# The fetch of the first pair's k, moved to the head of ScalarE's queue

## The chip, the cores and the metric

One core of one Trainium2 chip runs the whole kernel. The time is the device time of one execution in microseconds; lower is better.

## What is computed

Causal attention over 2 batches of 12 heads (448 positions, head dimension 64), then a gated layer and a hard-swish layer over the 896 rows of 768 that the attention gives. Cut to what matters:

```
scores = q @ k.T / sqrt(64);  scores above the diagonal = -1e9
attn   = exp(scores - max) / (sum + 1e-9)
x      = (attn @ v), heads side by side            # 896 x 768
x      = (sigmoid(x @ w_gate) * (x @ w_val)) @ w_out
h      = x @ w_in
out    = (h * clip(h + 3, 0, 6) / 6) @ w_out2
```

All inputs and the output are float32.

## The kernel before

The heads are handled in 12 pairs (6 for each batch). A pair p has its q, k and v fetched by `load(p, nm)` (L235); q and k come as two transfers each, one for each head, 112 KB every one, into a ring of three buffers (L246, L248). `t_pe` (L256) turns q and k by four transposes each on TensorE (L260) into PSUM; `t_out` (L267) copies them to SBUF, q on ScalarE with the scale (L270), k on VectorE (L272). The transposed q and k of all pairs share one PSUM buffer, except that the k of pair 0 goes to the buffer "pav" (L258). `s_pe` (L274) makes the scores: small mask products (L285), then the products s (L293), in two groups for each pair; `s_max`, `s_exp`, `s_rcp`, `s_nrm` are the softmax on VectorE, ScalarE and GpSimd; `c_pe` turns the probabilities (L347), and `d_pe` multiplies them with v (L367).

All engines take their instructions in the order in which the program names them. That order is a list of steps with planned times (`AT`, `SHIFT`, `OWN`, L397 to L422), sorted by `emit_in_order` (L515). Every transfer of q, k and v is issued by SP's queue, except pair 0's k, which is issued by ScalarE's (L248). In the planned order that step (`Lk` of pair 0) stands behind the scaling of pair 0's q (`Thq` of pair 0, L270). The steps Z (`z_pe`, L455) are products of ones into a PSUM tile that nobody reads; nine of them stand at the very beginning of TensorE's order (listed at L456 in the rows below), the others between the steps of the first pairs.

On SP's queue the order at the opening is: q of pairs 0, 1, 2, k of pair 1, q of pair 3, k of pair 2, v of pair 0, then on by pair; the first weights of the gated layer (`load_unit`, L98, L103) come after the v of pair 2. Their decoding begins with `dec_scale` (L113, L115) on ScalarE.

After the attention the gated layer (L190, L708) and the hard-swish layer (L190, L1161) follow, with weights fetched on SP's queue as buffers come free and decoded on ScalarE and VectorE; some of their split parts are made by transfers that GpSimd issues (L144).

Of the kernel before, what the change touches and what calls it, by code (L numbers as in the profile page):

```python
# [31 lines left out]
def kernel(  # L32
# [178 lines left out]
    with tc.manual_schedule():  # L211

        with ExitStack() as actx:
# [19 lines left out]
            live = {}  # L233

            def load(p, nm):  # L235
                b, hp = divmod(p, NPAIR)
                if nm == "v":
                    for j in range(2):
                        chunks = v[b, 2 * hp + j].rearrange("(c p) d -> p c d", p=D)
                        for x in range(2):  # L240
                            nc.sync.dma_start(
                                out=vs[p % NV][x * D : (x + 1) * D, x != j :, j],
                                in_=chunks[:, x != j :: 2],
                            )
                    return
                t = p_raw.tile([CP, S // CP, 2, D], F32, tag=nm, name=nm)  # L246
                for j in range(2):
                    (nc.scalar if (p, nm) == (0, "k") else nc.sync).dma_start(  # L248
                        out=t[:, :, j, :],
                        in_=(q if nm == "q" else k)[b, 2 * hp + j].rearrange(  # L250
                            "(c p) d -> p c d", p=CP
                        ),
                    )
                live[nm, p] = t
# [170 lines left out]
            for p in range(NP):  # L425
                def add(key, after, fn, *args):
                    steps.append(((p, key), [(p, a) for a in after], fn, (p, *args)))

                for nm in ("q", "k", "v"):
                    add("L" + nm, [], load, nm)  # L430
                for nm in ("q", "k"):
                    add("T" + nm, ["L" + nm], t_pe, nm)
                    add("Th" + nm, ["T" + nm], t_out, nm)
                for i, ts in enumerate(STILES):
                    add(f"S{i}", ["Thq", "Thk"], s_pe, ts)
                    for t in ts:
                        add(f"M{t}", [f"S{i}"], s_max, t)
                for ts in STILES:
                    for t in ts:
                        add(f"E{t}", [f"M{x}" for x in ts], s_exp, t)  # L440
                for i, ts in enumerate(STILES):
                    add(f"Q{i}", [f"E{t}" for t in ts], s_eps, i)
                    add(f"R{i}", [f"Q{i}"], s_rcp, i)
                    for t in ts:
                        add(f"N{t}", [f"R{i}"], s_nrm, t)
                for g in range(NG):
                    tiles = [f"N{t}" for t in range(GROUPS[g][0][0], NQ)]
                    add(f"C{g}", tiles, c_pe, g)
                    add(f"H{g}", [f"C{g}"], c_out, g)
                for d, gs in enumerate(DSTEPS):  # L450
                    add(f"D{d}", [*(f"H{g}" for g in gs), "Lv", *[f"D{d - 1}"][: d]], d_pe, d)
                add("Xh", [f"D{len(DSTEPS) - 1}"], x_hi)
                add("Xl", ["Xh"], x_lo)
# [61 lines left out]
            def emit_in_order():  # L515
# [19 lines left out]
                for key in sorted(left, key=lambda key: (when(key), key)):  # L535
                    _, fn, args = left[key]
                    fn(*args)

            ones = nc.const_aps.tensor(1.0, [P, 512], BF16)
            idle_ps = ps_pt.tile([P, 512], F32, tag="pt", name="pt")  # L540
            make_identity(nc, identf)
# [686 lines left out]
```

## Time and profile before

| what | us |
|---|---|
| median of three runs | 590.04 |
| lowest and highest run | 589.8, 591.88 |
| the profiled execution | 589.66 |
| its span, first to last instruction | 587.9 |

| engine | busy us | share of the span |
|---|---|---|
| TensorE | 573.8 | 98% |
| its weight loads | 506.1 | 86% |
| VectorE | 450.6 | 77% |
| ScalarE | 325.1 | 55% |
| GpSimd | 88.1 | 15% |

All times in the rows below are of the profiled execution, counted from the start of its span. In the profile PE is TensorE's products, PEld its weight loads, DVE is VectorE, ACT is ScalarE, POOL is GpSimd and SP is SyncE; SPq and ACTq are the issuing of transfers by those queues. L248 is line 248. Matmuls are pipelined and their ends are modelled, so neighbours may overlap by a little.

### The profile page before, as it was taken

Reading aid. Unit: us, or ns where it says so; the run is one execution under the profiler, and the core shown is the slowest. Engines: PE = TensorE matmul, PEld = TensorE weight load, DVE = VectorE, ACT = ScalarE, POOL = GpSimd, SP = SyncE. Lnnn points to the kernel's source line nnn. Section 1 sums busy time; section 2 is a strip of 40 time slices with the busy share of each in tenths; the row PEclk is TensorE's granted clock in tenths of the full one; section 3 lists DMA queues with packets and bytes.
Section 4 is the critical chain, followed back from the end, with each engine's and each line's share of the span. In section 5 each row is a group of like instructions: output and inputs, shape, how many; then the busy total and the mean of one; then the engine's idle time right before and its main releaser. Section 6 shows DMA issues by size and latency. Waiting matters only on the chain.

```text
span 587.9 us, 8611 instructions
## 1 busy us (share of the span) xinstructions
PE 573.8 (98%) x3252; PEld 506.1 (86%) x3253; DVE 450.6 (77%) x673; ACT 325.1 (55%) x619; POOL 88.1 (15%) x146
## 2 busy tenths in 40 slices
PE   6999999999999999999999999999999999999997
PEld 3666666899998999889999999988899899899997
DVE  1778995588778889889767887898999888867601
ACT  1988986454747565577343223777776644433200
POOL 0545455012201111110000000113122000000000
PEclk7999999999999999999999999999999999999999
DMA  7645625069848776761334533577988333338002
GB/s 150 155 118 132 146 67 177 2 157 216 212 131 193 180 208 168 198 180 31 108 115 154 162 107 108 145 179 187 216 191 224 94 107 110 107 109 255 0 3 92
DMA packets 86921, 82.21 MB, mean 140 GB/s; under 512 B 35680, under 2 KB 77408, under 8 KB 86880
## 3 DMA queue, kind: packets, MB, share of 16 engines
q1 hardware_dynamic: 79904, 64.27, 37.0%
q0 software_dynamic: 6048, 17.17, 15.9%
q8 instruction: 25, 0.41, 0.3%
q10 hardware_dynamic: 928, 0.23, 0.2%
q14 instruction: 16, 0.13, 0.1%
HBM read 61.73 MB, written 2.75 MB: 110 GB/s over the span
## 4 chain that ended last, share of the span: by engine, by line
PE 55%; DVE 29%; ACT 10%; issue 4%; DMA 2%; ACTq 0%; DVEq 0%
PE m L1161 17%; PE w L708 11%; PE m L190 10%; DVE b L128 5%; PE pav L367 5%; PE s L293 4%; PE pt L347 4%; DVE b L134 4%; DVE lo L158 3%; DVE b L124 3%; ACT hi L153 2%; ACT b L115 2%; PE tr L260 2%; DVE g L182 2%; DVE raw L120 2%
## 5 line engine op out<-in xcount | busy, mean ns | idle before, releaser
L1161 PE MATMUL m<-hi,g 128*128 128x384 f32 x448 | 114.3, 335 | 0.7 <-DVE g L1129 0.7
L153 ACT CAST hi<-b 128x768 fp32r<-128x768 f32 x36 | 29.8, 836 | 104.3 <-DVE b L134 96.3
L1161 PEld LDWEIGHTS m<-hi,g 128*128 128x128 f32 x448 | 80.8, 188 | 1.5 <-DVE g L1129 1.3
L1161 PE MATMUL m<-lo,g 128*128 128x384 f32 x224 | 74.9, 335 | 0.4 <-DVE lo L158 0.4
L708 PE MATMUL w<-T,hi 128*128 128x448 f32 x252 | 72.0, 367 | 1.4 <-ACT g2r L725 1.4
L190 PE MATMUL m<-g,hi 128*128 128x448 f32 x288 | 70.1, 365 | 0.0
L128 DVE SCALAR_TENSOR_TENSOR b<-b,raw 128x768 int32<-128x768 int32 x68 | 65.3, 960 | 2.3
L134 DVE SCALAR_TENSOR_TENSOR b<-raw,b 128x768 int32<-128x768 int32 x68 | 65.3, 960 | 2.4
L115 ACT ACTIVATE b<-raw 128x768 f32<-128x768 f32 x68 | 61.3, 905 | 0.0
L190 PEld LDWEIGHTS m<-g,hi 128*128 128x128 f32 x288 | 54.1, 188 | 4.3
L124 DVE TENSOR_SCALAR b<-b 128x768 f32<-128x768 f32 x68 | 37.9, 557 | 25.7 <-ACT b L115 25.3
L158 DVE TENSOR_TENSOR lo<-b,hi 128x768 fp32r<-128x768 f32 x36 | 34.2, 956 | 27.4 <-ACT hi L153 27.2
L337 POOL TENSOR_SCALAR pr<-pr,rc 128x192 f32<-128x192 f32 (+3 forms) x96 | 46.1, 497 | 53.0 <-DVE rc L329 43.9
L708 PEld LDWEIGHTS w<-T,hi 128*128 128x128 f32 x252 | 47.1, 188 | 5.9 <-ACT g2r L725 1.8
L190 PE MATMUL m<-x,hi 128*128 128x448 f32 x192 | 49.1, 368 | 0.0
L708 PE MATMUL w<-T,lo 128*128 128x448 f32 x126 | 46.3, 368 | 0.7 <-DMA lo<-S 0.5
L317 ACT ACTIVATE pr<-s,nm 128x192 f32<-128x192 f32 (+3 forms) x96 | 44.5, 476 | 3.7 <-DVE nm L305 3.2
L144 POOL DMA_DIRECT2D lo<-S x26 | 24.9, 956 | 131.4 <-ACT lo L143 111.2
L1161 PEld LDWEIGHTS m<-lo,g 128*128 128x128 f32 x224 | 42.0, 188 | 0.7 <-DVE lo L158 0.7
L305 DVE TENSOR_REDUCE nm<-s 128x2 f32<-128x384 f32 (+3 forms) x48 | 30.7, 681 | 14.9 <-PE s L293 14.5
L190 PE MATMUL m<-g,lo 128*128 128x448 f32 x144 | 41.0, 366 | 0.0
L190 PEld LDWEIGHTS m<-x,hi 128*128 128x128 f32 x192 | 35.7, 188 | 3.1 <-issue 0.4
(127 smaller groups left out, 1054.7 us busy)
## 6 DMA issues: line engine op xcount, KB each, us to landing
raw<-in_moe_w_out_dram SPq DMA_DIRECT2D x28, 768.0 KB, 4.4
raw<-in_moe_w_in_dram SPq DMA_DIRECT2D x16, 768.0 KB, 4.7
lo<-S POOLq DMA_DIRECT2D x26, 384.0 KB, 4.2
raw<-in_moe_w_gate_dram SPq DMA_DIRECT2D x12, 768.0 KB, 5.1
raw<-in_moe_w_val_dram SPq DMA_DIRECT2D x12, 768.0 KB, 5.3
q<-in_q_dram SPq DMA_DIRECT2D x24, 112.0 KB, 2.9
g<-b POOLq DMA_DIRECT2D x7, 384.0 KB, 6.5
k<-in_k_dram SPq DMA_DIRECT2D x22, 112.0 KB, 4.0
```

The source lines that it names most:

```text
L115: nc.scalar.activation(b, words(u)[0].bitcast(F32), AF.Copy, scale=REBIAS)
L124: nc.vector.tensor_scalar(b, b, UPPER_MAX, -UPPER_MAX, op0=ALU.min, op1=ALU.max)
L128: nc.vector.scalar_tensor_tensor(bi, bi, 3, words(u)[1], op0=ALU.logical_shift_left, op1=ALU.bitwise_or)
L134: nc.vector.scalar_tensor_tensor(bi, words(u)[0], -(2 ** 31), bi, op0=ALU.bitwise_and, op1=ALU.bitwise_or)
L153: nc.scalar.copy(hi, part_t[u])
L158: nc.vector.tensor_sub(lo, part_t.pop(u), split_t[u][0].bitcast(F32))
L190: nc.tensor.matmul(ps[:, b, :S], lhsT=w[a][:, i * P : (i + 1) * P], rhs=x(c, k0 + i, b), start=(first and i == 0 and n == 0), stop=(last a ...
L305: nc.vector.tensor_reduce(nm, live["s", p, t], axis=AX.X, op=ALU.max, negate=True)
L317: nc.scalar.activation(to if j else to[:, ::-1], ps[:, j].rearrange("p (c d) -> p c d", d=D), AF.Exp, bias=nm[:, j : j + 1], accum_out=sm[ ...
L337: nc.gpsimd.tensor_scalar(pr[:, j], pr[:, j], rc[:, j : j + 1], 1.0, op0=ALU.mult, op1=ALU.mult)
L708: nc.tensor.matmul(ps, lhsT=w[a][:, k * P : (k + 1) * P], rhs=x[:, c, i], start=(first and i == 0 and n == 0), stop=(i == HK - 1 and n == ...
L1161: nc.tensor.matmul(po[t], lhsT=g2[2 * s + i][a][:, t * P : (t + 1) * P], rhs=w[e][:, i * HC : (i + 1) * HC], start=(s == 0 and i == 0 and ...
```

## The change

`load` returns at once when the asked q or k tile is already live, and pair 0's k is loaded ahead of everything else that the attention part emits, before the constants are made and before the planned order begins. When the planned step for it comes, it does nothing. The issuing queue is ScalarE's, as before.

```diff
@@ -234,6 +234,8 @@
             def load(p, nm):
                 b, hp = divmod(p, NPAIR)
+                if (nm, p) in live:
+                    return
                 if nm == "v":
@@ -536,6 +538,7 @@
                     _, fn, args = left[key]
                     fn(*args)
 
+            load(0, "k")
             ones = nc.const_aps.tensor(1.0, [P, 512], BF16)
             idle_ps = ps_pt.tile([P, 512], F32, tag="pt", name="pt")
             make_identity(nc, identf)
```

## Rows read from the trace of the kernel before

**Rows 1.** The page's forty slices: TensorE's busy tenths and its granted clock.
```profile
PE   6999999999999999999999999999999999999997
...
PEclk7999999999999999999999999999999999999999
```

**Rows 2.** Chain that ended last, 0 to 18 us: start us, us, what.
```profile
0.78 3.58 PE pt L456 x9
4.36 0.48 PE tr L260 x4
...
5.36 4.02 DMA k<-in_k_dram
...
9.42 1.01 PE tr L260 x4
10.43 0.43 PE pt L456
10.86 0.75 PE tr L260 x4
11.60 0.43 PE s L285 x8
12.04 1.87 PE s L293 x8
13.90 0.60 PE tr L260 x4
...
14.73 1.06 PE s L293 x8
...
16.49 0.81 PE pt L456 x3
...
17.32 0.35 PE s L285 x8
17.67 0.95 PE s L293 x8
```

**Rows 3.** Stretches of one us: busy us by engine, granted clock, DMA share, GB/s.
```profile
4.00:5.00 1.00, 0.82 (x6) 0.39 (x4) 0.00 (x0) 0.14 (x1) 0.00 (x0) 1.00 0.88 199
...
7.00:8.00 1.00, 0.00 (x0) 0.00 (x0) 0.00 (x0) 0.00 (x0) 0.00 (x0) 0.60 1.28 287
...
13.00:14.00 1.00, 1.00 (x5) 0.17 (x2) 0.05 (x1) 0.00 (x0) 0.00 (x0) 0.50 0.67 151
14.00:15.00 1.00, 1.00 (x16) 0.86 (x18) 1.00 (x2) 0.00 (x0) 0.00 (x0) 0.99 0.99 222
```

**Rows 4.** Timeline: start us, us, engine, line, operation, output<-input, count [idle before, releaser].
```profile
0.74 1.28 ACT L270 ACT_TABLE_LOAD   x1 [0.74 <-PEq L1212]
...
3.84 1.02 SPq L248 DMA_DIRECT2D k<-in_k_dram  x2
...
4.87 0.99 ACTq L248 DMA_DIRECT2D k<-in_k_dram  x2
...
10.47 0.62 DVE L272 COPY kt<-tr 128x448 f32<-128x448 f32 x1 [7.25 <-PE tr L260]
...
22.00 0.61 SPq L103 DMA_DIRECT2D raw<-in_moe_w_gate_dram  x1
...
34.09 0.91 ACT L115 ACTIVATE b<-raw 128x768 f32<-128x768 f32 x1
```

**Rows 5.** Transfers, single ones: count, KB each, us to landing (last row: median).
```profile
q<-in_q_dram SPq DMA_DIRECT2D x1, 112.0 KB, 2.9
...
k<-in_k_dram SPq DMA_DIRECT2D x1, 112.0 KB, 3.3
k<-in_k_dram ACTq DMA_DIRECT2D x1, 112.0 KB, 3.6
...
raw<-in_moe_w_gate_dram SPq DMA_DIRECT2D x12, 768.0 KB, 5.1
```

**Rows 6.** Waits for transfers, 15 to 588 us, longest: total us, times, longest us.
```profile
PEld w L708 <- DMA lo<-S: 0.9, 1, 0.9
```

## The prediction

> **What bounds the kernel now.** I read the page's forty slices first. TensorE's granted clock is full in every slice but the first, and the first is also the only slice, apart from the end, in which TensorE is less than 90% busy [rows 1]. So the place to look is the opening, 14.7 us long, and the views for it are the chain that ended last, the one-microsecond stretches, and the timeline of the queues.
>
> The chain of the opening [rows 2] reads: nine warm-up products to 4.36, the four transposes of pair 0's q (0.48 us), the scaling of qt on ScalarE, then 4.02 us of one transfer, the second half of pair 0's k, and only at 9.42 the transposes of that k. From there the chain is TensorE without a hole, step after step, into the first products s (L293) and on into pair 1 and pair 2. That transfer is late for one reason: ScalarE's queue issues k's two halves at 4.87, in 0.99 us, right when the ScalarE instruction that stands before them starts, and that one waits for q's transposes [rows 4]. ScalarE's own work until then is one table load at 0.74 [rows 4].
>
> The second thing to see is the clock. In the stretch 7 to 8 us, where TensorE does nothing, the mean granted clock is 0.60, and 14 to 15 has 0.99; 13 to 14 still 0.50, and 4 to 5 reads full [rows 3]. Half is the 1.2 GHz level, full the 2.4 GHz level. The warm-up products had ended in a full clock, as q's transposes (0.48 us) against k's (1.01 us) show [rows 2]; the engine then stood idle for 4.6 us and lost it, and did the first 4.5 us of work, from 9.42 to 13.90, at half.
>
> **The change part by part.** (1) Two transfers of 112 KB are issued at the head of ScalarE's queue instead of behind the scaling of qt; the planned load of that tile then returns at once, since it is live. No instruction is added or taken away. The issue costs 0.99 us of ScalarE's queue [rows 4], from 0.74 to 1.73. The table load (1.28 us) then runs to about 3.0, and ScalarE's next instruction needs q's transposes, which end at 4.84 [rows 2]; so this costs nothing, and would cost only if q's transposes ended before 3.0. GpSimd and SP issue nothing later for it. SP's queue is not passed by any other transfer of its own, but its first ones now share the DMA engines with k.
>
> (2) When k lands. The second half is issued at 0.74 + 0.49 = 1.23. Lower bound: the second half of pair 0's q, issued at about the same time on SP with an empty machine, took 2.9 us [rows 5], so 4.1. Upper bound: the same transfer of before, with SP issuing beside it as now, took 4.02 us [rows 2] (its first half 3.6 [rows 5]), so 5.25. By sharing, q itself may slip by as much. In the good case q's transposes run as before and k's start right behind them, at 4.85; in the bad case both inputs land at 5.25, q's transposes take 0.5 to 0.6, and k's start at 5.85. Neither row is clearly nearer (the first has the empty machine, the second the two queues), so I take the middle, 5.3. Against 9.42 that is **4.1 us** off the path (3.6 to 4.6).
>
> (3) What the clock gives. With k there, TensorE's hole shrinks from 4.6 us to under 1 us, and I expect the clock to stay full. Then the chain from 9.42 to 13.90 [rows 2] runs at the durations that the same groups have after 14 us: transposes 0.60 instead of 1.01 (k) and 0.75 (pair 1's q); one warm-up product 0.27 (0.81 for three) instead of 0.43; mask products 0.35 instead of 0.43; eight products s 0.95 instead of 1.87. That is 2.77 instead of 4.48, so **1.7 us** more. VectorE's copy to kt (0.62 us [rows 4]) lies beside it: it ends 0.60 + 0.66 = 1.26 after k's transposes start, and the products s want it after 0.60 + 0.27 + 0.60 + 0.35 = 1.82. If the clock is not kept, this term is nothing.
>
> (4) What is late next. Pair 1's k, which SP issues from 3.84 [rows 4]. Its second half, issued about 4.36, took 3.3 us [rows 5] and lands at 7.7; its transposes would be due at 5.3 + 2.77 = 8.1. It fits with 0.4 to spare; at 4.02 us it would land at 8.4 and cost 0.3. Everything later on SP has more room. As the worst case, the first gate weights, were they issued no earlier than now (22.00) [rows 4], land after 5.1 [rows 5] at 27.7, and ScalarE's first use of them, at 34.09 now, comes at 28.3 [rows 4].
>
> (5) Whether the shift reaches the end. All engines take their work in order and every step of pair 1 stands behind one of pair 0; there is no later wait of TensorE on a transfer from memory. The longest wait on any transfer after 15 us is 0.9 us, and it is for a copy that GpSimd issues inside the GLU [rows 6], which moves with the rest. So the sum is 4.1 + 1.7 = 5.8 us, all of it on the path: 589.66 - 5.8 = 583.9 for the profiled execution (span 587.9 and 1.8 around it). That execution lies 0.4 below the median of the runs, 590.04, from which the forecast is **584.2**; its own range is 583.2 to 584.7, from 3.6 + 1.7 to k1 just in time (5.8 + 1.0).
>
> One rule of the Trainium skill speaks against a part of this. The rows show 199 GB/s between 4 and 5 us, with SP's queue at work almost alone, and 287 GB/s between 7 and 8, with ScalarE's beside it [rows 3], so a second queue did move more. The page "DMA: Bandwidth & Descriptors", section "Issuing engines are not separate DMA queues", says that transfers of all engines run on the same 16 DMA engines and interleave, so that issuing from several saves only sequencer time. By that rule q and k of pair 0 would slow each other; this is the first rival.
>
> **The rivals.** *The two fetches slow each other.* If two queues move no more than one, k's 224 KB beside q's cost 1.1 us at 199 GB/s [rows 3], q lands at 4.1 + 1.1 = 5.2 and k's transposes start at 5.85: 3.6 + 1.7 = 5.3 off, **584.7**. For it: q and k compete from the first byte. Against it: the 287 GB/s.
>
> *The clock falls all the same.* Between 4.4 and 8 us TensorE does transposes, one warm-up product and the first products s, with small holes, and not the dense work that it had before 14 us. If it runs at half from k's transposes on, as now, only term 2 is won: 590.04 - 4.1 = **585.9**. For it: no row of before shows a full clock through such a thin stretch. Against it: from 15 us on the chain has the same steps and the clock stays [rows 1].
>
> *The change doesn't do what it says.* The table load could stay ahead of the two issues, for its place is not written in the code. Then k is issued 1.28 us later [rows 4], lands at 5.4 to 6.5, and some 1.1 us of the gain is gone: **585.3**.
>
> *The wait is hidden anyway.* Some transfer or engine that does not depend on pair 0 sets a later point, and all of the shift is given back there: **590.0**. Against it stands the absence of any long wait on a transfer after 15 us [rows 6].
>
> *Slower.* The clock falls early, and the thin opening, no longer followed by 4.5 us of dense work, does not lift it for two pairs. At half rate a group of products s costs about 0.9 more (1.87 against 0.95) and four transposes about 0.4 more [rows 2]; a pair has two of each, so 2.6. The 4.1 us of term 2 are eaten when half rate outlasts the rest of pair 0 (one s and one transpose group, 1.3) and the whole of pair 1 (2.6); through pair 2 as well it would be 1.3 + 2.6 + 2.6 = 6.5 lost, 590.04 - 4.1 + 6.5 = **592.4**. Against it: half rate has ended here after 4.6 us of work.
>
> **How the numbers follow.** Forecast 584.2: 0.53. Fetches slow each other, 584.7: 0.15. Clock falls, 585.9: 0.16. Table load first, 585.3: 0.07. Hidden, 590.0: 0.05. Slower, 592.4: 0.04. The range 583.2 to 586.5 takes in the first four with their bounds and leaves out 0.09 above and a little below. A measurement of this kernel can tell about 0.5%, 2.95 us, from no change: faster 0.91, within 0.5% 0.05, slower 0.04.
>
> **What would show it.** Step 1: k's two issues at 0.74 on ScalarE's queue, ahead of the table load. Step 2: k's transposes between 4.85 and 5.85. Step 3: a granted clock of 1.00 in every stretch from 5 to 15 us, the first eight products s in about 1 us and ending near 8. Step 4: no wait for pair 1's k. Step 5: the later pairs spaced as now, all 5.8 us earlier, and the chain's other rows unchanged. I am wrong in the size if the clock row reads half there, and wrong in the matter if later pairs stand where they stood.

## The result, and the profile after

On the chip of the prediction's runs the changed kernel takes 583.76 us (median; 583.12 to 584.82) against 590.25 before: a ratio of 0.9887, interval 0.9862 to 0.9912. The profiled execution takes 583.4 against 589.66. The forecast was 584.2.

The chain of the opening in the changed kernel, start us, us, what; it answers to [rows 2]:

```profile
0.74 3.19 DMA k<-in_k_dram
...
3.94 0.39 SPq L250
...
4.37 3.79 DMA k<-in_k_dram
...
8.30 0.57 PE tr L262 x4
...
10.15 0.53 PE tr L262 x4
...
11.91 0.95 PE s L295 x8
```

The 4.02 us of pair 0's k are gone from the chain. In their place stands another k, pair 1's: its second half is issued at 4.37, lands after 3.79 us, and its transposes start at 8.30. In the kernel before they started at 13.90, so the chain is 5.60 us earlier there, and 5.76 at the first products s of pair 1 (11.91 against 17.67). By the first two links, SP's issue of pair 1's k waited for the landing of pair 0's first half of k. The trace bears this out: the issue waits on the semaphore that tells of this landing, and goes out 0.02 us behind it. It costs nothing here: the second half, for which the transposes wait, is issued at 4.37, and was issued at 4.38 in the kernel before.

The timeline of the same stretch, columns as in [rows 4]:

```profile
0.74 1.01 ACTq L250 DMA_DIRECT2D k<-in_k_dram  x2
0.78 4.00 PE L458 MATMUL pt<-const-bfloat16-1.0 128*128 128x512 bf16 x9 [0.78 <-PEq L1215]
1.78 1.28 ACT L272 ACT_TABLE_LOAD   x1 [1.78 <-issue]
4.60 0.98 PE L262 MATMUL tr<-identf,q 112*128 112x112 f32 x4
5.38 0.92 PE L262 MATMUL tr<-identf,k 112*128 112x112 f32 x4
6.35 0.55 PE L262 MATMUL tr<-identf,q 112*128 112x112 f32 x4
7.01 1.13 PE L295 MATMUL s<-kt,qt 64*128 64x192 f32 x8
8.30 0.57 PE L262 MATMUL tr<-identf,k 112*128 112x112 f32 x4 [0.15 <-DMA k<-in_k_dram]
```

Pair 0's k is issued first of all on ScalarE's queue, with the table load behind it. Its transposes follow q's directly, at 5.38. The first four transposes of q and of k take 0.98 and 0.92 us, which is half rate, and from 6.35 on the same group takes 0.55: in this execution the clock rose at about 6.1, where in the profiled execution of before it had risen by 4.3. The eight products s take 1.13 instead of some 2 us.

Stretches of one us, columns as in [rows 3]:

```profile
5.00:6.00 1.00, 1.00 (x8) 1.00 (x7) 0.00 (x0) 0.38 (x1) 0.00 (x0) 1.00 1.32 217
7.00:8.00 1.00, 1.00 (x16) 0.64 (x10) 0.00 (x0) 0.47 (x1) 0.00 (x0) 1.00 1.20 207
13.00:14.00 1.00, 1.00 (x7) 0.45 (x6) 1.00 (x2) 1.00 (x6) 0.90 (x2) 1.00 0.83 187
```

TensorE is busy throughout but for the 0.15 us before pair 1's k, and the clock column stays at 1.00 where before it read 0.50 from 7.2 to 14. It reads 1.00 in 5 to 6 as well, while the transposes ran at half rate: ahead of the first change that it records, the column shows no level to be trusted.

Whether the shift reaches the end is read from the 68 decoding steps of VectorE on L128, which are spread over the whole kernel. The first, the 26th and the 27th of them, in the kernel before:

```profile
44.41 0.96 DVE L128 SCALAR_TENSOR_TENSOR b<-b,raw 128x768 int32<-128x768 int32 x1
...
257.75 0.96 DVE L128 SCALAR_TENSOR_TENSOR b<-b,raw 128x768 int32<-128x768 int32 x1
...
279.37 0.96 DVE L128 SCALAR_TENSOR_TENSOR b<-b,raw 128x768 int32<-128x768 int32 x1
```

and in the changed kernel:

```profile
38.65 0.96 DVE L128 SCALAR_TENSOR_TENSOR b<-b,raw 128x768 int32<-128x768 int32 x1
...
251.94 0.96 DVE L128 SCALAR_TENSOR_TENSOR b<-b,raw 128x768 int32<-128x768 int32 x1
...
273.19 0.96 DVE L128 SCALAR_TENSOR_TENSOR b<-b,raw 128x768 int32<-128x768 int32 x1
```

The shift is 5.76 at the first, 5.81 at the 26th and 6.18 at the 27th; it stays between 6.18 and 6.27 up to the last. So between these two traces 5.76 us come from the opening, nothing of it is given back, and 0.4 more appears in one stretch of the gated layer that the change does not touch. That stretch turns up in the experiments.

### The profile page after: what moved, and what is told of

Same layout as the page of the kernel before. It is cut to its first block, busy times and chain, and to the rows that moved or that the text cites. A ratio compares the mean times of both kernels' runs of the same rounds, so it can differ in the third digit from the quotient of the medians.

```text
span 581.6 us, 8612 instructions
## 1 busy us (share of the span) xinstructions
PE 572.2 (98%) x3253; PEld 505.4 (87%) x3253; DVE 450.5 (77%) x673; ACT 324.8 (56%) x619; POOL 88.4 (15%) x146
## 4 chain that ended last, share of the span: by engine, by line
PE 58%; DVE 28%; ACT 8%; issue 3%; DMA 2%; SPq 0%; ACTq 0%; DVEq 0%; POOLq 0%
PE m L1164 17%; PE w L711 15%; PE m L190 10%; DVE b L128 5%; PE pav L369 5%; PE pt L349 4%; PE s L295 4%; DVE b L134 4%; DVE lo L158 3%; DVE b L124 3%; ACT hi L153 2%; DVE g L182 2%; ACT b L115 2%; DVE raw L120 2%; PE tr L262 1%
## 5 line engine op out<-in xcount | busy, mean ns | idle before, releaser
L128 DVE SCALAR_TENSOR_TENSOR b<-b,raw 128x768 int32<-128x768 int32 x68 | 65.3, 960 | 2.3
```

Source lines behind the costliest of these rows:

```text
L128: nc.vector.scalar_tensor_tensor(bi, bi, 3, words(u)[1], op0=ALU.logical_shift_left, op1=ALU.bitwise_or)
```

## The experiments

In what follows "the first step" is the start of the first L128 step. It measures the opening alone: 44.41 in the kernel before, 38.65 in the changed one.

**The changed kernel again.**

> The changed kernel again, as the reference for the other runs on the same chip. Its first trace had pair 0's k transposed from 5.38 us and pair 1's k from 8.30, with a wait of 0.15 us for the transfer of pair 1's k. If the time of the opening is set by that transfer (theory), pair 1's k is again transposed within 0.2 us of 8.3, whatever the clock does before, and the time is 583 to 585. If it is set by the clock and the products (rival), an execution whose clock rises sooner has it up to 1 us earlier.

584.31 us (583.33 to 584.43) against 589.56 for the kernel before on that chip, ratio 0.9910 (0.9896 to 0.9923). The first step is at 38.73 and pair 1's k is transposed from 8.29. The clock rose late here too (q's transposes 0.98 us), so theory and rival were not told apart. The stretch between the 26th and the 27th step of L128, however, differs from the first trace of the very same code:

```profile
252.09 0.96 DVE L128 SCALAR_TENSOR_TENSOR b<-b,raw 128x768 int32<-128x768 int32 x1
...
274.24 0.96 DVE L128 SCALAR_TENSOR_TENSOR b<-b,raw 128x768 int32<-128x768 int32 x1
```

It is 22.15 us here and was 21.25 there. Up to it the two executions differ by 0.15 us, behind it by 1.05. Against the first trace of the kernel before, the shift is 5.68 at the first step here and 5.36 at the last. The medians differ likewise: they fell by 6.49 us on the first chip and by 5.25 on this one. So the opening has to be read from the opening, not from the total time.

**The kernel before, a second trace.**

> The kernel before once more, for a second trace of its opening. If the moment at which the clock first rises differs between executions of the same code (theory, from the traces so far: q's transposes took 0.57 us for four in the first trace of before and 0.95 to 0.98 in three others), then either q's transposes again take 0.57 and end at 4.8, with k's at 9.4, or they take 0.95 and end at 5.5, with k's at 10.0; the time from there to the first eight products s of pair 1 is 8.0 to 8.4 in both, since TensorE then stands idle for over 4 us. Rival (the moment is fixed by the code): 4.8 and 9.4 again.

One execution, 590.63 us. In its chain:

```profile
4.78 0.64 PE tr L260 x4
...
5.44 0.39 ACT qt L270
...
5.87 4.00 DMA k<-in_k_dram
...
9.91 1.01 PE tr L260 x4
...
12.53 1.87 PE s L293 x6
...
18.34 0.95 PE s L293 x8
```

The moment of the first rise does differ between executions of one code. Here q's transposes took 0.83 us and ended at 5.42, so the scaling of qt, the issue of k behind it and k's transposes came 0.5 us later than in [rows 2]; the first step is at 45.05, 0.64 later. From k's transposes to pair 1's first products s it is 8.43 us (8.25 in the first trace, 8.0 to 8.4 expected), at half rate again. In the kernel before, then, a late clock delays the fetch; in the changed one it cannot. Against this trace the changed kernel's opening is 6.40 us earlier. The stretch of the gated layer is 21.24 us here and was 21.62 in the first trace.

**Only the clock: the gap filled, the fetch where it was.**

```diff
+            WARM += [-76841.5] * 18
             OWN.update({f"Z{i:02}": at for i, at in enumerate(WARM)})
```

> The kernel before, with the fetch of pair 0's k where it was, but 18 more idle products put between q's and k's transposes of pair 0, so that TensorE doesn't stand still for 4.6 us. Only the clock's term is tried. Theory: k's transposes still start at 9.4, the clock reads full from there on, the stretch from them to pair 1's k takes 2.8 to 3.0 us instead of 4.48, and the time is 1.5 to 1.7 below the kernel before, 588.6. Rival: the clock is worth nothing, since the data sets the pace of the opening: same time as before. A second rival: the filling overruns the landing of k and eats the gain.

> The kernel before with the 18 idle products in the gap, for a second trace, to see whether the opening's gain is steady and where it was lost. Theory: from k's transposes to the first eight products s of pair 1 again 6.2 us, 2.0 less than in the kernel before; decoding steps up to 250 us are 1.4 to 2.0 earlier than in the kernel before, by one constant shift; what the time then shows differs by up to 0.8 because the 108 products of the gated layer's last pair take 22.2 to 23.3 us from one execution to the next. Rival: the idle products make the gated layer slower, and the shift shrinks in every trace of this kernel by 0.5 or more.

In the first trace of it the chain reads:

```profile
6.01 3.99 DMA k<-in_k_dram
...
10.04 0.61 PE tr L260 x4
...
11.53 1.00 PE s L293 x8
...
16.27 0.95 PE s L293 x8
```

From k's transposes to pair 1's first products s it is 6.23 us, and 6.22 in the second trace (16.11 - 9.89): 2.0 less than 8.25 and 2.2 less than 8.43. The clock term is real in the opening. The filling itself did not get in the way: its products ended at 9.50 and 9.76, before k landed at 10.00 and 9.85. But k's transposes came late, at 10.04 and 9.89, since the clock rose late in both executions, and the first step is at 43.02 and 42.85: 1.4 to 1.6 before the first trace of before, 2.0 to 2.2 before the second. The time does not show it: 589.25 (587.79 to 592.44) against 589.56, ratio 0.9995 (0.9980 to 1.0009); the one execution of the second trace took 588.98. Part of the loss is in the same stretch, 22.08 and 22.02 us here. That is no longer than the 22.15 of the unfilled changed kernel, so the filling is not shown to cause it, but two traces do not exclude it either: at the last step of L128 only 0.65 and 0.66 us are left against the first trace of before (1.66 and 1.67 against the second), as the rival of the second trace wanted. For the time of this kernel the theory is not confirmed.

**Only the fetch: no idle products at the head.**

```diff
             WARM = [
-                -183075, -183075, ... (nine of them), -76840.5,
+                -76840.5,
```

> The changed kernel without the nine idle products at the head of TensorE's order, so k's fetch is early but the opening's work starts on a cold engine. Theory: q's transposes at 4.5 and k's at 5.4 as with the change, but the first products s at half rate (1.9 us for eight), so that pair 1's k is transposed at about 9.9 instead of 8.3; the time is 1.2 to 1.7 above the changed kernel, about 585.3, still 4.5 to 5 below the kernel before. Rival (the clock doesn't matter, transfers set the opening): 583.8 as with the change.

585.22 us (584.55 to 585.38), ratio 0.9925 (0.9912 to 0.9939), 0.9 above the changed kernel on the same chip, where 1.2 to 1.7 was expected; the opening shows more. Its chain:

```profile
1.19 3.30 DMA q<-in_q_dram
...
4.62 1.73 PE tr L262 x8
...
7.96 1.87 PE s L295 x8
9.83 0.88 PE tr L262 x4
```

q's and k's transposes stand where the changed kernel has them, the eight products s take 1.87 us, and pair 1's k is transposed from 9.83 (expected: 9.9). The first step is at 40.38, 1.73 after the changed kernel's. So with the early fetch alone the opening gains 4.03, and the clock is worth 1.73 on top: the two terms of the sum, measured apart.

**Place or queue: k first, on SP.**

```diff
-                    (nc.scalar if (p, nm) == (0, "k") else nc.sync).dma_start(
+                    nc.sync.dma_start(
```

> The changed kernel with pair 0's k still ahead of everything, but on SP's queue, before q of pair 0. It tells the place in the order from the second queue. Theory (most of the gain is the place, a queue of its own adds SP's issue time): k lands by 4, q's second half is issued at 2.3 and lands at 5.3 to 5.6, q's transposes at 5.6, k's at 6.2; pair 1's k is issued 1.0 us later and lands at 9.2, so its transposes start at 9.2 to 9.3 instead of 8.3: 0.9 to 1.0 slower than the changed kernel, 4.7 faster than before. Rival (the second queue saves only sequencer time, which is small beside the transfer): within 0.3 us of the changed kernel.

583.61 us (583.28 to 583.96), ratio 0.9891 (0.9874 to 0.9907): by time not to be told from the changed kernel. The first step is at 39.21, 0.56 after the changed kernel's and 5.20 before the old one's. q's transposes start at 5.15 and k's at 5.93, as late as q's landing:

```profile
2.24 2.78 DMA q<-in_q_dram
...
5.15 1.71 PE tr L262 x8
```

My theory wanted 0.9 to 1.0, because pair 1's k is issued 1.0 us later; it is (4.91), but its transposes start at 8.64, when the products s are done, without a wait. On one queue each transfer lands sooner after its issue (2.78 us for this one; in the changed kernel q's second half took 3.3 and pair 1's k 3.8). So nine tenths of the opening's gain is the place in the order, and a queue of its own gives at most 0.56 us. How much of the 0.56 is the queue is not shown, since here k also stands ahead of q, and q's second half, issued at 2.24 instead of 1.19, landed at 5.02 instead of 4.46. The order q, then k, all on SP, was not run. An estimate for it: in the kernel before, the fourth transfer on SP's queue landed at 5.10; k's second half in that place would land 0.1 us later than in the changed kernel (5.00). The Trainium skill's rule ("DMA: Bandwidth & Descriptors", section "Issuing engines are not separate DMA queues", that a second queue saves only sequencer time) agrees with this: SP spends 0.93 us on issuing k here, and 0.56 is less.

**Pair 1's k on ScalarE's queue too.**

```diff
-                    (nc.scalar if (p, nm) == (0, "k") else nc.sync).dma_start(
+                    (nc.scalar if p < 2 and nm == "k" else nc.sync).dma_start(
...
             load(0, "k")
+            load(1, "k")
```

> The changed kernel with pair 1's k fetched by ScalarE's queue too, right behind pair 0's. Theory (pair 1's k was the next thing late): its second half is issued at about 2.3 instead of 4.4 and lands by 6.5, the wait of 0.15 us before its transposes is gone, and they start when the first products s are done, at 8.1 with a clock like that of the first trace and at 7.3 to 7.6 if the clock rises sooner; time 0.2 to 0.9 below the changed kernel. Rival: the earlier traffic slows q and k of pair 0 by as much as pair 1's k gains: pair 0's k transposed 0.3 to 0.5 later and no gain or a small loss.

583.58 us (583.5 to 584.43), ratio 0.9904 (0.9891 to 0.9918). By the median it lies 0.7 below the changed kernel on the same chip, as the theory wanted, but not by the opening: the stretch between the 26th and the 27th step is 21.25 us here and was 22.15 there. In the opening the rival was nearer, though at another transfer. The wait for pair 1's k is gone, but a new one stands in its place:

```profile
4.60 0.57 PE L262 MATMUL tr<-identf,q 112*128 112x112 f32 x4 [0.30 <-DMA q<-in_q_dram]
5.08 0.57 PE L262 MATMUL tr<-identf,k 112*128 112x112 f32 x4
6.86 0.57 PE L262 MATMUL tr<-identf,q 112*128 112x112 f32 x4 [0.99 <-DMA q<-in_q_dram]
```

Pair 1's q, with more traffic beside it, took 4.49 us instead of 3.8, and its transposes started at 6.86 instead of 6.35. The first step is at 39.20, 0.55 later than with the change. SP's queue waited too: the issue of its next transfer, pair 2's q, went out only when pair 0's first half of k had landed at 3.94. SP's own waits up to 6 us have it:

```profile
SPq L250 <- DMA k<-in_k_dram: 1.2, 1, 1.2
```

One thing more is seen here: the clock rose early (q's and k's transposes 0.57), TensorE then waited 0.99 us, and all groups after that still ran at full rate.

**Pair 1's k ahead of pair 2's q on SP.**

```diff
             load(0, "k")
+            load(0, "q")
+            load(1, "q")
+            load(1, "k")
```

> The changed kernel with pair 1's k issued by SP ahead of pair 2's q instead of behind it, so that fewer bytes stand before it. Theory (the opening is now set by the order in which bytes land): its second half is issued at 3.3 and lands at 7.0 to 7.3 instead of 8.2; its transposes start when the first products s are done: 8.1 if the clock rises late, 7.3 to 7.6 if early. Decoding steps up to 250 us 0.15 to 0.8 earlier than in the changed kernel; time 583.0 to 583.8. Rival: nothing gained, because the first products s, not the transfer, set the start in every execution.

583.28 us (583.03 to 583.42), ratio 0.9887 (0.9872 to 0.9901). Pair 1's k no longer makes anybody wait, and is transposed from 8.11, as expected for a late clock. Yet the first step is at 38.70, not earlier than with the change: the chain now leaves TensorE for VectorE.

```profile
7.24 0.97 PE s L295 x8
...
8.23 1.29 DVE nm L307 x2
9.52 0.54 DVE kt L274
...
10.11 0.60 PE tr L262 x4
```

The next transposes need the PSUM buffer that VectorE's copy to kt frees, and that copy stands behind the maxima of pair 0: 10.11 against 10.08 in the changed kernel (by its timeline; the chain above has 10.15). The time lies within the 583.0 to 583.8 of the theory, but the opening gained nothing. The rival (nothing gained) held, for a reason that neither had named. No variant is shown to beat the changed kernel.

**The fetch held back.**

```diff
             nc.vector.tensor_copy(maskb, maskf)
+            held = const.tile([P, 1], F32, name="held")
+            nc.scalar.copy(held, maskb[:, :1])
+            load(0, "k")
```

(and the call ahead of the constants taken out)

> The changed kernel with the two issues of pair 0's k held back on ScalarE's queue until the mask is made (by a small copy of one column of it), so that they go out at about 2.3 us instead of 0.74; nothing else is moved. What does a microsecond of delay of this fetch cost? Theory: the second half is issued at 2.8, lands at 6.6 after 3.8, k's transposes start at 6.65 instead of 5.38 (1.3 later), the clock stays full after its rise, the first products s follow 1.5 us behind, and decoding steps up to 250 us come 1.0 to 1.4 later than in the changed kernel, 4.4 to 4.7 earlier than in the kernel before; about 585.0. Second effect to look for: in the changed kernel SP's issue of pair 1's k followed within 0.02 us of the landing of pair 0's first half of k (3.92). If it waits for that transfer (a shared completion counter), it now goes out at 5.5 instead of 3.9, pair 1's k lands at 9.5 to 9.8 and takes its place as what is late last, 1.4 later than before; if not, it goes out at 3.9 again. Rival: no cost, since q's transposes and the clock's rise at 6 us set the pace anyway: within 0.3 us of the changed kernel.

585.47 us (583.74 to 586.62), ratio 0.9918 (0.9893 to 0.9943). The two issues went out at 2.26 and 2.96, 1.5 and 1.8 us late, and the first step is at 41.74, 3.09 after the changed kernel's. Both theory (1.0 to 1.4) and rival missed it. The chain, the timeline, then the stretches:

```profile
0.74 2.20 DMA q<-in_q_dram
...
2.96 4.18 DMA k<-in_k_dram
```

```profile
4.18 0.55 PE L262 MATMUL tr<-identf,q 112*128 112x112 f32 x4
7.19 1.01 PE L262 MATMUL tr<-identf,k 112*128 112x112 f32 x4 [2.46 <-DMA k<-in_k_dram]
...
9.62 1.57 PE L295 MATMUL s<-kt,qt 64*128 64x192 f32 x8
```

```profile
6.00:7.00 1.00, 0.00 (x0) 0.00 (x0) 0.00 (x0) 0.00 (x0) 0.00 (x0) 1.00 1.36 214
7.00:8.00 1.00, 0.81 (x5) 0.78 (x6) 0.00 (x0) 0.00 (x0) 0.00 (x0) 0.58 1.38 209
```

In this execution the clock had risen early; TensorE was then idle for 2.46 us until k landed, the clock fell to half and rose again in 10 to 11 (0.71). So a second half issued 1.8 us late cost 1.8 in k's transposes, and 1.3 more by the clock: this is the prediction's "clock falls all the same", brought about by the delay. This holds for the traced execution, which took 585.97 us. Another took 586.62, with the same mean granted clock of 0.997; the other two took 584.97 and 583.74 at 1.000, and whether the clock fell in them is not shown.

The other question is not settled by this run. SP issued pair 1's k at 3.85, before pair 0's first half had landed (5.20), so here it does not wait for that transfer. But the semaphores in the traces show that the two programs wait for different transfers. In each of the five traces with pair 0's k first on ScalarE's queue, one issue of SP waits on the semaphore of pair 0's first half and goes out 0.02 us behind its landing; in the changed kernel it is the issue of pair 1's k. Here that issue waits for no transfer; instead pair 0's second half waits for q's first half, which landed at 2.94. That is why it went out at 2.96 and not at the 2.8 expected.

## Why the prediction was right

**The issue costs nothing** (step 1): as put, but for one thing: SP does issue something later for it, pair 1's first half of k, by 0.1 us (3.94 against 3.84) and without cost. The two issues stand at 0.74, the table load at 1.78 to 3.06, and ScalarE's next work at 5.62. The rival of a table load that stays ahead fell with this row.

**When k lands** (step 2): the number held, 4.04 us instead of 4.1 (5.38 against 5.3), the reason only in part. k's second half, issued at 1.19, took 3.8 and landed at 5.0, inside the bounds of 4.1 and 5.25. What set 5.38 was q's transposes, which ran at half rate behind warm-up products that took 4.00 us instead of 3.58. q's second half did take 3.3 us instead of the 2.9 of [rows 5], but that cost the path next to nothing: its transposes start at 4.60, and at 4.57 in the second trace of before and with the gap filled, where q had landed by 3.85 and 3.51. That the number held is in part luck: a hold-up that I had not reckoned with, the late clock, put k's transposes near the middle of the bounds that I had drawn for the landing. I had reckoned with a clock that is full by 4.4 because the one trace of before showed it. Over the ten traces with the warm-up products q's four transposes took 0.55 to 0.57 us in three, 0.83 in one and 0.95 to 0.98 in six.

**What the clock gives** (step 3): 1.7 forecast. From k's transposes to pair 1's k the chain takes 2.92 us instead of 4.48, so 1.56, with 0.15 of waiting in it and k's own transposes still at half rate; taken alone it is 1.73. The mechanism is shown from three sides: with the head cold the gain is gone, with the gap filled the opening has it without the fetch, and with a gap of 2.46 us 1.3 of it is lost again.

**What is late next** (step 4): the right transfer, with its margin wrong. I gave pair 1's k 0.4 us to spare, with 3.3 us of flight; with pair 0's k and q flowing together it took 3.8 and was 0.15 late. My upper bound (4.02 us, 0.3 late) covers it. That VectorE's copy to kt stands beside it I had not seen; the run with pair 1's k earlier shows that it sets the next transposes by itself (10.11 against 10.08), so the 0.15 us cost nothing further on.

**The shift reaches the end** (step 5): right. It is constant at 5.75 to 5.81 over the first 26 of 68 steps. The rest of the 6.3 us between the two spans is no work of the change: the stretch between the 26th and 27th step took 21.62 and 21.24 us in two executions of the kernel before, 21.25 and 22.15 in two of the changed one. The forecast of 5.8 is to be held against 5.76 in the opening; that the profiled time fell by 6.26 is 0.4 of luck in that stretch and 0.1 elsewhere.

**The rivals.** That the fetches slow each other is true by 0.4 us for q and 0.5 for pair 1's k, not by 1.1. My argument against it, the 287 GB/s, was one stretch of 1 us: from 2 to 8 us the changed kernel moved 220 GB/s and the run with SP's queue alone 204. The clock did not fall, and the run with the 0.99 us hole shows some margin; with the fetch held back, and a hole of 2.46 us, it does fall. Of the slower case, a clock that stays down for two pairs, nothing was seen: with k's fetch at the head half rate ended by 10.7 us even without the warm-up products.

## What to carry to other kernels

A transfer that the first work needs should not stand, in its queue's order, behind an instruction that itself waits for another input: the place in the order was worth 5.2 us here, the choice of queue 0.56 at most. A hole in TensorE's opening is priced twice, once as a wait and once by what runs at half rate behind it, and both prices can be read from one trace by taking the same groups before and after the clock's rise. When a fetch is moved forward, reprice the transfers that now share the engines with it, and read the gain from a stretch near the change, because later stretches may vary by more than the terms in question.

## What the runs showed of the hardware that was not expected

The same opening code, with dense products from 0.78 us on, had its clock up before 4 us in some executions (nine warm-up products in 3.52 to 3.58 us instead of 4.00) and only at about 6.7 in another (k first on SP: k's transposes from 5.93 on still at half rate), and the granted-clock column reads 1.00 from the start in all of them; only the durations (0.43 us for a warm-up product, 0.98 against 0.57 for four transposes) show the half rate.

In the opening a transfer of 112 KB took 2.2 to 3.0 us from issue to landing with SP's queue alone at work and up to 4.8 with two (pair 1's k on ScalarE's queue), while the total rate from 2 to 8 us hardly differed: 204 GB/s with SP alone, 220 in the changed kernel.

An issue can wait for the landing of a transfer that it has no use for, because it takes over that transfer's semaphore. It cost nothing in the changed kernel and held the issue of pair 2's q back by 1.2 us in the run with both k on ScalarE's queue.

The 108 products in the gated layer's last stretch were one piece of 22.64 us in one execution of the kernel before and 22.24 in another, at a granted clock of 1.00 in both. What sets this was not tried and stays open.
